# Two expert blocks at 240 columns, an earlier normalisation of 16 rows, and a conditional block laid out behind its empty side

## The chip, the cores and the metric

One core of a Trainium2 chip runs the kernel. The time is device time in microseconds of one execution; the number that counts is the median of several. The profile is of one execution. Its engines are PE (TensorE, matrix products), DVE (VectorE), ACT (ScalarE), POOL (GpSimd, here mostly indirect DMAs) and SP (SyncE, which issues the weight loads). In the profile, a "q" behind an engine's name means its instruction queue.

## The reference

A pre-norm block: linear attention with a residual, then a mixture of experts of which each token uses one, with a residual. S = 2048 tokens, D = 512, 32 heads, F = 1792, E = 8 experts, all in f32.

```python
h  = x + attention(layernorm(x), wqkv, w_phi, wo)
xf = layernorm(h)
idx = argmax(xf @ w_gate)              # one expert for each token; its gate is softmax of one value, 1
out = zeros_like(xf)
for e in range(E):
    out = out + (idx == e) * (silu(xf @ w1[e]) @ w2[e])
return h + out
```

With the inputs of this case the experts 0 to 7 get 103, 594, 80, 127, 286, 222, 239 and 397 tokens.

## The kernel before

The attention is computed first. While it ends, tables are built that say which rows belong to which expert; then the experts are worked through in **stages**, each with one expert's weights. Rows are fetched from DRAM by indirect DMAs on POOL (`rows`), normalised on DVE or ACT (`norm`, `tile_n`), transposed on PE into columns (`turn`, `tile_t`), multiplied by w1 (called g1 here), passed through Silu, multiplied by w2 (g2), added to the residual (`result`) and scattered to the output.

Every product is made of three matmuls in fp32r (`mm3`), of a high and a low part of each operand: hi x hi, lo x hi, hi x lo. High parts are rounded copies made by ACT (`hi_of`, `hi_piece`), low parts are differences made by DVE (`lo_of`, `lo_piece`). The weights of an expert come in seven chunks of 1 MB into the buffers `raw[0]` to `raw[6]`, loaded by SP's queue, and are split piece by piece into `whi` and `wlo`. A `step(c, i)` in a stage's table of hooks is such a piece i of chunk c.

The stages run in this order: unit 0 (128 rows of the most loaded expert, the "star", number 1), wide S (its other 468 rows), **pair 1** and **pair 2** (256 rows each), pairs 3 to 8 (only as many as the tables call for), a wide stage of WN = 288 rows, single(0), wide U with WU = 400 rows, single(1), and singles 2 to 7, again conditional. Here wide U holds expert 7, the 288-row stage expert 4, the pairs experts 5 and 6, and the singles experts 0, 2 and 3. Pairs 3 to 8 do not run, and one conditional single does.

A pair has 14 steps j over F (NJ) and one more. In step j, g1 makes 128 rows of the hidden layer for all 256 columns of x: four k blocks of D, three matmuls each, the weights stationary and x moving. Silu on ACT and the split on ACT and DVE follow, and two steps later g2 adds their product with w2 to two halves `pl[0][:, t, :]` in PSUM, with 128 rows of tokens stationary and 512 columns of w2 moving. `todo[j]` holds what else is put into a step: gathers of the next pair, normalisations, steps of weight splitting, and the branch hint.

`tbl` is a generator that computes the tables in wide S on DVE, one part to a hook (`behind(next, tbl)`): which expert fills the wide stages (`o1`, `o0`), how many blocks each expert needs, and where the rows lie. The functions star_a to star_d behind it write the index lists, read the expert numbers into registers and issue the loads of the next unit (`load(c, nx0)`).

Order is set in three ways. Each engine runs its instructions in order. A scheduler puts them into that order by the sequence of the code and by `after(...)`, which orders but is no wait on another engine. Waits come from the data: a semaphore for each buffer's reader and writer. For a conditional block both sides are laid out in program memory, the preferred one right behind the compare; the empty side sets the semaphores as if the block had run.

In single(0), the rows of the coming wide U are prepared between pieces of g2: `tile_n(t)` normalises tile t on DVE, `tile_t(t)` transposes it on PE and splits it into `zx`. Tile 3 has 16 rows (400 - 384), gathered into `xg[0]`.

Of the kernel before, what the change touches and what calls it, by code (L numbers as in the profile page):

```python
# [41 lines left out]
ST = ((0, P), (P, P), (2 * P, P), (3 * P, WS - 3 * P))  # L42
WC = 20
# [7 lines left out]
EV = E + 1  # L51
# [7 lines left out]
def kernel(  # L59
# [62 lines left out]
    V.tensor_scalar(first[:, 1:EV], desc8, -float(NT), float(NT * E), op0=OP.mult, op1=OP.add)  # L122
# [17 lines left out]
    est1 = consts.tile([P, 1], F32, name="est1")  # L140
# [6 lines left out]
    lemask = consts.tile([P, EV, EV], F32, name="lemask")  # L147
# [30 lines left out]

    def gather(q):
        for t in range(2):  # L180
            rows(xg[2 * (q == 1) + t], 2 * q + t)
# [14 lines left out]
    def norm(g, eng, xn=None):  # L196
        xn = xn2[0] if xn is None else xn
        if eng is A:
            return A.activation(xn[:, 0:D], g[:, 0:D], AF.Identity, bias=g[:, D:D + 1], scale=g[:, D + 1:D + 2])
        return V.tensor_scalar(xn[:, 0:D], g[:, 0:D], g[:, D + 1:D + 2], g[:, D:D + 1], op0=OP.mult, op1=OP.add)  # L200

    def turn(h, l, pool=None, xn=None):
        xn = xn2[0] if xn is None else xn
        pt = pool.tile([P, 512], F32, name="mtx", tag="s") if pool else bank("mtr")
        for k in range(KD):
            pin["mtr"] = T.transpose(pt[:, k * P:(k + 1) * P], xn[:, k * P:(k + 1) * P], ident)
        ptv = pt.rearrange("p (k t) -> p k t", k=KD)
        i = hi_of(h, ptv)
        return i, lo_of(l, ptv, h)

    def turn2(q, t, pool=None):
        v = slice(t * P, (t + 1) * P)
        return turn(xhi[1 - q % 2][:, :, v], xlo[1 - q % 2][:, :, v], pool)
# [78 lines left out]
    def tables(pool):  # L292
# [9 lines left out]
        key, m8 = v8("key"), v8("m8")  # L302
        V.tensor_copy(te, ns)
        for w, o in ((WU, o1), (WN, o0)):
            V.tensor_scalar(bs, cnt, P / 2 - 0.25 - w, FLOOR, op0=OP.add, op1=OP.add)
            V.scalar_tensor_tensor(b8, bs, FLOOR, starP, op0=OP.subtract, op1=OP.max)
            V.tensor_tensor(d8, ns, b8, op=OP.subtract)
            V.tensor_tensor(key, d8, desc8, op=OP.add)
            if o is o0:
                V.scalar_tensor_tensor(key, o1, -4.0 * S, key, op0=OP.mult, op1=OP.add)  # L310
            V.max(out=m8, in_=key)
            V.tensor_scalar(o, key, m8[:, 0:1], None, op0=OP.is_ge)
            V.tensor_tensor(d8, d8, o, op=OP.mult)
            pin["lo"] = V.tensor_tensor(te, te, d8, op=OP.subtract)
            if o is o1:
                yield
        yield
        t2, pe, pn, w8, n8 = [v8(n) for n in ("t2", "pe", "pn", "w8", "n8")]
        tp, more = one("tp"), one("more")
# [6 lines left out]
        w9 = pool.tile([P, EV], F32, name="w9")  # L326
        V.scalar_tensor_tensor(ns, n8, 1.0, star, op0=OP.mult, op1=OP.mult, accum_out=nb[:, 0:1])
        V.tensor_tensor(nb[:, 1:EV], n8, ns, op=OP.subtract)
        V.tensor_reduce(tp, pn, AX.X, OP.add)
        V.scalar_tensor_tensor(more, nS, 2.0 * PT, tp, op0=OP.mult, op1=OP.subtract)  # L330
        V.scalar_tensor_tensor(nb[:, 0:1], more, 0.0, nb[:, 0:1], op0=OP.max, op1=OP.add)
        V.scalar_tensor_tensor(bs, w8, 1.0, star, op0=OP.mult, op1=OP.mult, accum_out=w9[:, 0:1])
        pin["lo"] = V.tensor_tensor(w9[:, 1:EV], w8, bs, op=OP.subtract)
# [79 lines left out]
    def flags_of(pool):  # L413
        one = lambda name: pool.tile([P, 1], F32, name=name)
        ex, junk = tb["ex"], tb["junk"]
        end = endx[:, 1:EV + 1]
        live, ce, eend, nx, cc, md, c1, own_ = [one(n) for n in ("live", "ce", "eend", "nx", "cc", "md", "c1", "ow")]
        eI = pool.tile([P, E], F32, name="eI")
        ew = pool.tile([P, 2], F32, name="ew")
        fm = tb["sT"]  # L420
        V.tensor_scalar(eI, desc8, -1.0, float(E), op0=OP.mult, op1=OP.add)
        V.tensor_scalar(c1, ex, 0.0, est1, op0=OP.is_equal, op1=OP.mult)
        V.tensor_scalar(live, pol, end[:, EV - 1:EV], None, op0=OP.is_lt)
        for i in range(2):
            V.scalar_tensor_tensor(jk, (o0, o1)[i], 1.0, eI, op0=OP.mult, op1=OP.mult, accum_out=ew[:, i:i + 1])
        V.scalar_tensor_tensor(junk[:, 0:EV], end, po, onesE[:, 0:EV], op0=OP.is_equal, op1=OP.mult, accum_out=ce)
        V.scalar_tensor_tensor(junk[:, 0:EV], slots[:, 0:EV], ex, end, op0=OP.is_equal, op1=OP.mult, accum_out=eend)
        V.tensor_tensor(own_, c1, ex, op=OP.add)
# [3 lines left out]
        V.tensor_scalar(fm[:, 96:97], own_, 1.0, float(E - 1), op0=OP.subtract, op1=OP.min)  # L432
# [18 lines left out]
    with ExitStack() as actx:  # L451
# [608 lines left out]
        def s_star():  # L1060
# [8 lines left out]
            V.tensor_scalar(est1, m[:, 1:2], -1.0, float(E + 1), op0=OP.mult, op1=OP.add)  # L1069
            V.tensor_scalar(est16, m[:, 1:2], float(-NT), float(E * NT), op0=OP.mult, op1=OP.add)  # L1070
            V.tensor_scalar(first[:, 0:1], m[:, 1:2], float(-NT), float(E * NT + 4), op0=OP.mult, op1=OP.add)
# [274 lines left out]
    def pair_result():  # L1346
        for t in range(2):
            result(LC + 1 + t, pl[0][:, t, :], xg[2 + t])
# [9 lines left out]
    def result(col, py, g):  # L1358
        pin["y"] = V.scalar_tensor_tensor(g[:, 0:D], py, g[:, D + 2:D + 3], g[:, 0:D], op0=OP.mult, op1=OP.add)  # L1359
        scatter(g, col)  # L1360
# [66 lines left out]
    def pair(q, hooks=None):  # L1427
# [6 lines left out]
        py = []  # L1434

        def g2(i, t):
            v = slice(t * P, (t + 1) * P)
            with after(pin["g1"]):
                pin["g2"] = mm3(py[t], rh[i % 3][:, v], rl[i % 3][:, v], w2_at(whi, i), w2_at(wlo, i), i == 0, i == NJ - 1)

        def ahead(t):
            with after(pin["hi"]), after(pin["lo"]):
                pin["lo"] = norm(xg[t], V)
# [66 lines left out]
    def single(r):  # L1510
# [55 lines left out]
        if r == 0:  # L1566
# [6 lines left out]
            with after(h2), after(x2):  # L1573
# [114 lines left out]
    def star_n(t):  # L1688
        with after(pin["lo"]):
            pin["lo"] = norm(xg[2 + t], V)  # L1690

    def star_x(t):
# [5 lines left out]
        3: [behind(next, tbl), star_a], 4: [star_b, star_c], 5: [star_f, star_d] + [call(rows, xrS[t], t, ST[t][1], gidS) for t in range(3)],  # L1698
# [19 lines left out]
    with ExitStack() as ictx:  # L1718
        for q in range(3, NP + 1):
            ictx.enter_context(tc.If(np_v > 2 * (q - 1), preferred_fallthrough_block=True, label=f"p{q}"))  # L1720
# [16 lines left out]
    pair_result()  # L1737
# [77 lines left out]
```

## Time and profile before

| what | value |
|---|---|
| time, median of 3 runs | 625.16 us (624.47 to 625.37) |
| the profiled execution: its time, its span, its mean clock | 624.18 us, 622.5 us, 0.998 |
| pair 1, first matmul to the next stage's first | 353.7 to about 396.2 us |
| pair 2 | about 396.2 to 438.5 us |
| wide stage of 288 rows | 438.5 to 483.8 us |
| single(0) | 483.8 to 509.5 us |
| matmul rows of g1 in the two pairs, 128x256 | 6 groups of 56 |

A timeline row of the profile reads: start in us, duration in us, engine, line of the kernel, operation, what is written <- what is read, shapes, type and count, and in brackets how long the engine stood idle before it and what released it. Rows of one line give the duration in ns (least, median, most) and the first and last start. In a by-form row the numbers behind the bar are the busy time in us and the mean duration in ns. Durations of matmuls overlap, since the next one starts while the last drains; the distance between starts is what a matmul costs.

### The profile page before, as it was taken

The numbers are of one execution on the slowest core, as the hardware profiler recorded it, in microseconds if no ns is written. First come the engines' busy times: TensorE is split into PE (matmuls) and PEld (weight loads), VectorE is DVE, ScalarE is ACT, GpSimd is POOL, SyncE is SP. The second block draws the span as 40 slices with busy tenths as digits, with TensorE's granted clock in tenths as the row PEclk, the third lists the DMA queues.
The fourth block names the chain that finished last, engine by engine and source line by source line (L and its number), as shares of the span: only waits on it lengthen the run. The fifth ranks groups of instructions, "written<-read, shape, count | busy, mean of one in ns | idle before, by whom it ended". The sixth has DMA issues, their size and how long they took to land. (4 is left out here: it accounts for less than half of the span.)

```text
span 622.5 us, 13751 instructions
## 1 busy us (share of the span) xinstructions
PE 612.6 (98%) x5213; PEld 549.1 (88%) x5213; DVE 437.5 (70%) x902; ACT 355.5 (57%) x626; POOL 238.9 (38%) x333
## 2 busy tenths in 40 slices
PE   9999999999999999999999999999999999999996
PEld 8888888888889999888888999989999879999884
DVE  7988786878898878985434657776555784446992
ACT  6666766667534537872234546666456655645781
POOL 5587788877706645541200012230401430010420
PEclk9999999999999999999999999999999999999999
DMA  8712111210103249631294276574756584444930
GB/s 312 265 37 54 50 53 52 53 52 20 35 10 96 81 153 386 232 80 51 76 411 135 68 287 264 199 249 148 263 177 195 179 303 158 135 170 143 339 126 20
DMA packets 25118, 95.20 MB, mean 153 GB/s; under 512 B 3844, under 2 KB 3844, under 8 KB 17872
## 3 DMA queue, kind: packets, MB, share of 16 engines
q1 hardware_dynamic: 20624, 80.81, 37.1%
q0 software_dynamic: 4272, 13.38, 6.6%
q8 instruction: 44, 0.72, 0.5%
q14 instruction: 34, 0.28, 0.1%
q10 hardware_dynamic: 144, 0.02, 0.0%
HBM read 85.77 MB, written 8.68 MB: 152 GB/s over the span
## 5 line engine op out<-in xcount | busy, mean ns | idle before, releaser
L244 DVE TENSOR_TENSOR wlo<-raw,whi 128x1024 fp32r<-128x1024 f32 (+1 forms) x119 | 135.2, 1159 | 25.2 <-ACT whi L87 24.7
L87 ACT ACTIVATE whi<-raw 128x1024 fp32r<-128x1024 f32 (+1 forms) x120 | 115.0, 992 | 3.2 <-issue 1.6
L176 POOL DMA_INDIRECT xg<-hbuf,gidx x26 | 32.4, 1246 | 124.7 <-DVE xn L200 49.2
L93 PE MATMUL gw<-zx,whi 128*128 128x256 f32 (+3 forms) x212 | 69.8, 329 | 0.0
L699 POOL TENSOR_TENSOR ph<-t,sm 128x1024 f32<-128x1024 f32 x32 | 62.1, 1942 | 16.9 <-DVE sm L697 16.5
L95 PE MATMUL gw<-zx,wlo 128*128 128x256 f32 (+3 forms) x212 | 68.6, 323 | 0.0
L94 PE MATMUL gw<-zx,whi 128*128 128x256 f32 (+3 forms) x212 | 68.5, 323 | 0.0
L90 DVE TENSOR_TENSOR hA<-hs,hA 128x256 fp32r<-128x256 f32 (+3 forms) x57 | 27.2, 478 | 58.6 <-ACT hA L87 56.7
L1313 ACT ACTIVATE hs<-gw 128x468 f32<-128x468 f32 (+2 forms) x39 | 19.2, 493 | 76.2 <-PE gw L95 73.9
L93 PE MATMUL yt<-hA,whi 128*128 128x468 f32 (+2 forms) x168 | 56.7, 338 | 0.0
L95 PE MATMUL yt<-hA,wlo 128*128 128x468 f32 (+2 forms) x168 | 56.7, 338 | 0.0
L696 DVE TENSOR_REDUCE sm<-t 128x64 f32<-128x1024 f32 x32 | 38.9, 1215 | 20.0 <-ACT t L691 18.0
L691 ACT ACTIVATE t<-t,rstd 128x1024 f32<-128x1024 f32 x32 | 36.8, 1151 | 27.2 <-DVE t L690 24.7
L93 PEld LDWEIGHTS gw<-zx,whi 128*128 128x128 f32 x212 | 39.9, 188 | 2.1 <-ACT hs L1313 0.4
L94 PEld LDWEIGHTS gw<-zx,whi 128*128 128x128 f32 x212 | 40.0, 189 | 1.5
L95 PEld LDWEIGHTS gw<-zx,wlo 128*128 128x128 f32 x212 | 39.9, 188 | 1.3
L190 POOL DMA_INDIRECT out_dram<-xg,sidx x13 | 14.5, 1119 | 65.7 <-DVE xg L1359 31.4
L94 PE MATMUL yt<-hA,whi 128*128 128x288 f32 (+2 forms) x116 | 37.8, 326 | 0.0
L93 PE MATMUL po<-wohi,xh 128*128 128x260 f32 x128 | 37.5, 293 | 0.1
L95 PE MATMUL po<-wohi,xl 128*128 128x260 f32 x128 | 36.6, 286 | 0.1
L94 PE MATMUL po<-wolo,xh 128*128 128x260 f32 x128 | 36.1, 282 | 0.0
L87 ACT ACTIVATE hA<-hs 128x256 fp32r<-128x256 f32 (+3 forms) x70 | 33.8, 483 | 2.2
(466 smaller groups left out, 1785.9 us busy)
## 6 DMA issues: line engine op xcount, KB each, us to landing
raw<-in_w_dram SPq DMA_DIRECT2D x56, 1024.0 KB, 6.6
xt<-in_x_dram SPq DMA_DIRECT2D x32, 256.0 KB, 3.1
xT<-in_xTs_dram SPq DMA_DIRECT2D x16, 256.0 KB, 2.7
hbuf<-hb SPq DMA_DIRECT2D x6, 515.0 KB, 4.5
hbuf<-hb SPq DMA_DIRECT2D x2, 514.0 KB
phT<-in_wv_dram SPq DMA_DIRECT2D x4, 256.0 KB, 3.3
phT<-in_wqkT_dram SPq DMA_DIRECT2D x4, 256.0 KB, 5.5
phT<-in_wqkT_dram SPq DMA_DIRECT2D x2, 512.0 KB
```

The lines of the kernel that those rows point to most:

```text
L87: return A.activation(dst, src, AF.Copy)
L90: return V.tensor_tensor(dst, src, hi.bitcast(F32), op=OP.subtract)
L93: T.matmul(ps, ahi, bhi, start=first, stop=False)
L94: T.matmul(ps, ahi, blo, start=False, stop=False)
L95: return T.matmul(ps, alo, bhi, start=False, stop=last)
L176: G.indirect_dma_start(out=dst[0:n, :], out_offset=None, in_=hbuf if col or tab is gidS else hbuf[0:S // 2, :], in_offset=bass.IndirectOff ...
L190: m = G.indirect_dma_start(out=out, out_offset=bass.IndirectOffsetOnAxis(ap=tab[0:n, col:col + 1], axis=0), in_=src[0:n, 0:D], in_offset=N ...
L244: return eng.tensor_tensor(lo, r, h.bitcast(F32), op=OP.subtract)
L691: pin["ex"] = A.activation(t, t, AF.Exp, scale=st[c]["rstd"])
L696: V.tensor_reduce(sm, t, AX.X, OP.add)
L699: pin["f2"] = G.tensor_tensor(ph.rearrange("p (a f) -> p a f", f=DH), t, bc(sm, DH), op=OP.mult)
L1313: A.activation(h, p, AF.Silu)
```

## The change

There are four parts.

**240 columns.** A constant PN = 240 is added, and pairs 1 and 2 pass 240 columns instead of 256: 128 and 112 rows. Gathers, normalisations, transposes, g1, Silu, splits, the second half of g2 and the results shrink to that (`pair_n`). In pair 2 the last 32 rows of the second half of `pl` are set to zero at its start.

**The tables.** So that two experts fit into 240, the tables choose them as they choose those of the wide stages: two more rounds of the loop over (WU, o1), (WN, o0), now also (PN, o2), (PN, o3), with a running `used`. The lists grow by three entries (EV = E + 4), the experts are named by a table `eid`, and the tables need one hook more, so star_a to star_d each stand one step later. The mask `lemask` is no longer a constant made at the start but a scratch tile in `raw[0]`, made on POOL at the end of the attention. For the inputs here the two experts are 5 and 6, as before, and the number of blocks of every kind is unchanged.

**Late rows.** In single(0), `tile_n(3)` stands before the split of chunk 0 instead of behind tile 2.

**The conditional pair 3.** The If of pair 3 prefers the empty side behind the compare, and its hint is inverted to match.

The core of the diff:

```diff
+PN = 240
-EV = E + 1
+EV = E + 4
...
+    def pair_n(q, t):
+        return (PN if q < 3 else PT) - P if t else P
...
-        for w, o in ((WU, o1), (WN, o0)):
+        for w, o in ((WU, o1), (WN, o0), (PN, o2), (PN, o3)):
...
-            if o is o0:
-                V.scalar_tensor_tensor(key, o1, -4.0 * S, key, op0=OP.mult, op1=OP.add)
+            if o is not o1:
+                V.scalar_tensor_tensor(key, used, -4.0 * S, key, op0=OP.mult, op1=OP.add)
...
+        V.scalar_tensor_tensor(key, te, 1.0 / P, first[:, 4:EV], op0=OP.mult, op1=OP.add)
+        for i, o in enumerate((o2, o3)):
+            V.scalar_tensor_tensor(bs, o, 1.0, key, op0=OP.mult, op1=OP.mult, accum_out=w9[:, 1 + i:2 + i])
+            pin["lo"] = V.scalar_tensor_tensor(b8, o, 1.0, eid[:, 4:EV], op0=OP.mult, op1=OP.mult,
+                                               accum_out=eid[:, 1 + i:2 + i])
...
-                f"p{q + 1}", hint=smin(smax(vals["p"] - 2 * q, 0), 1),
+                f"p{q + 1}", hint=smin(smax(2 * q + 1 - vals["p"] if q == 2 else vals["p"] - 2 * q, 0), 1),
...
+        if q == 2:
+            V.memset(pl[0][P - 32:P, 1, :], 0.0)
...
-                        pin["g1"] = mm3(p, w1_at(whi, c, k)[:, o:o + P], w1_at(wlo, c, k)[:, o:o + P], own_x[0][:, k, :],
-                            own_x[1][:, k, :], k == 0, k == KD - 1)
+                        pin["g1"] = mm3(p, w1_at(whi, c, k)[:, o:o + P], w1_at(wlo, c, k)[:, o:o + P], own_x[0][:, k, 0:nc_],
+                            own_x[1][:, k, 0:nc_], k == 0, k == KD - 1)
...
                 h2, x2 = tile_t(0, ws[0], xU, UT)
-            with after(h2), after(x2):
+            with after(x2):
+                n = tile_n(3, ws[3], UT)
+            with after(h2), after(n):
                 split_chunk(0)
...
                 h2, x2 = tile_t(2, ws[2], xU, UT)
-                with after(pin["lo"]):
-                    tile_n(3, ws[3], UT)
...
-        3: [behind(next, tbl), star_a], 4: [star_b, star_c], 5: [star_f, star_d] + [call(rows, xrS[t], t, ST[t][1], gidS) for t in range(3)],
+        3: [behind(next, tbl)], 4: [behind(next, tbl), star_a], 5: [star_b, star_c], 6: [star_f, star_d] + [call(rows, xrS[t], t, ST[t][1], gidS) for t in range(3)],
...
-            ictx.enter_context(tc.If(np_v > 2 * (q - 1), preferred_fallthrough_block=True, label=f"p{q}"))
+            ictx.enter_context(tc.If(np_v > 2 * (q - 1), preferred_fallthrough_block=q > 3, label=f"p{q}"))
```

How it moves instructions is seen in the order of the program, where a row is a line, an operation, what it writes <- what it reads, and a shape. On PE, at the end of pair 2, before: the last g2, the compare for pair 3, and then the body of pair 3.

```order
L93 MATMUL pl<-whi_4553,hA 128x512
L94 MATMUL pl<-wlo_4554,hA 128x512
L95 MATMUL pl<-whi_4553,hA 128x512
L1718 COMPARE_AND_BRANCH
L1254 UNCONDITIONAL_BRANCH
L1256 UNCONDITIONAL_BRANCH
```

Now the compare is followed by the empty side, which ends with a branch, and the body of pair 3 comes behind it:

```order
L94 MATMUL pl<-whi_4554,hA 112x512
L95 MATMUL pl<-wlo_4555,hA 112x512
L96 MATMUL pl<-whi_4554,hA 112x512
L1735 COMPARE_AND_BRANCH
L1735 UNCONDITIONAL_BRANCH
L1268 UNCONDITIONAL_BRANCH
L1270 UNCONDITIONAL_BRANCH
```

The other end of both jumps lies some 1,780 such rows further on PE, behind the bodies of pairs 3 to 8, at the first matmul of the 288-row stage. Before, the seven branches that end the innermost body and the six empty sides stood there, pair 3's the last of them:

```order
L93 MATMUL pl<-whi_4553,hA 128x512
L94 MATMUL pl<-wlo_4554,hA 128x512
L95 MATMUL pl<-whi_4553,hA 128x512
L1718 UNCONDITIONAL_BRANCH x7
L93 MATMUL mh<-zx,whi_3702 128x288
```

Now six branches are left at that place; the empty side of pair 3, whose branch goes to the same matmul, is the one that was shown behind the compare. The other engines have the same layout.

On DVE, in single(0), before: `zx` 128x4x128 are the low parts of tiles 0 to 2, the row 16x512 is `tile_n(3)`, `wlo` are weight pieces, and `zx` 128x4x16 is tile 3.

```order
L90 TENSOR_TENSOR zx<-mtr,zx 128x4x128
L244 TENSOR_TENSOR wlo_3703<-raw_3524,whi_3702 128x1024 x2
L90 TENSOR_TENSOR zx<-mtr,zx 128x4x128
L244 TENSOR_TENSOR wlo_3709<-raw_3527,whi_3708 128x1024
L90 TENSOR_TENSOR zx<-mtr,zx 128x4x128
L1279 TENSOR_SCALAR xg_3710<-xg_3710 16x512
L90 TENSOR_TENSOR zx<-mtr,zx 128x4x16
```

Now:

```order
L91 TENSOR_TENSOR zx<-mtr,zx 128x4x128
L1293 TENSOR_SCALAR xg_3711<-xg_3711 16x512
L251 TENSOR_TENSOR wlo_3704<-raw_3524,whi_3703 128x1024 x2
L91 TENSOR_TENSOR zx<-mtr,zx 128x4x128
L251 TENSOR_TENSOR wlo_3710<-raw_3527,whi_3709 128x1024
L91 TENSOR_TENSOR zx<-mtr,zx 128x4x128
L91 TENSOR_TENSOR zx<-mtr,zx 128x4x16
```

The 16x512 row has moved ahead of three weight pieces and of tiles 1 and 2; nothing else changed its place there.

More of the change, by code (lines that the diff above doesn't have):

```diff
@@ L121 @@
     first = consts.tile([P, EV], F32, name="first")
-    V.tensor_scalar(first[:, 1:EV], desc8, -float(NT), float(NT * E), op0=OP.mult, op1=OP.add)
+    V.memset(first[:, 0:3], 0.0)
+    V.tensor_scalar(first[:, 4:EV], desc8, -float(NT), float(NT * E), op0=OP.mult, op1=OP.add)
+    eid = consts.tile([P, EV + 1], F32, name="eid")
+    V.tensor_scalar(eid[:, 4:EV], desc8, -1.0, float(E), op0=OP.mult, op1=OP.add)
+    V.memset(eid[:, EV:EV + 1], 0.0)
     blk0 = consts.tile([P, EV + 1], F32, name="blk0")
@@ L177, in rows @@
                              in_offset=bass.IndirectOffsetOnAxis(ap=tab[0:n, col:col + 1], axis=0))
+    def pair_n(q, t):
+        return (PN if q < 3 else PT) - P if t else P
     def gather(q):
         for t in range(2):
-            rows(xg[2 * (q == 1) + t], 2 * q + t)
+            rows(xg[2 * (q == 1) + t], 2 * q + t, pair_n(q, t))
     def own(r):
@@ L204, in turn @@
         pt = pool.tile([P, 512], F32, name="mtx", tag="s") if pool else bank("mtr")
+        n = h.shape[2]
         for k in range(KD):
-            pin["mtr"] = T.transpose(pt[:, k * P:(k + 1) * P], xn[:, k * P:(k + 1) * P], ident)
-        ptv = pt.rearrange("p (k t) -> p k t", k=KD)
+            pin["mtr"] = T.transpose(pt[:, k * n:(k + 1) * n], xn[0:n, k * P:(k + 1) * P], ident[0:n, 0:n])
+        ptv = pt[:, 0:KD * n].rearrange("p (k t) -> p k t", k=KD)
         i = hi_of(h, ptv)
@@ L211, in turn2 @@
     def turn2(q, t, pool=None):
-        v = slice(t * P, (t + 1) * P)
+        v = slice(t * P, t * P + pair_n(q, t))
         return turn(xhi[1 - q % 2][:, :, v], xlo[1 - q % 2][:, :, v], pool)
@@ L301, in tables @@
         V.scalar_tensor_tensor(ns, ns, FLOOR, starP, op0=OP.subtract, op1=OP.max)
-        key, m8 = v8("key"), v8("m8")
+        key, m8, used, o2, o3 = [v8(n) for n in ("key", "m8", "used", "o2", "o3")]
+        w9 = pool.tile([P, EV], F32, name="w9")
+        V.memset(w9[:, 0:1], 0.0)
+        lemask = pool.tile([P, EV, EV], F32, name="lemask")
+        G.memset(lemask, 1.0 / P)
+        G.affine_select(out=lemask, in_=lemask, compare_op=OP.is_ge, fill=0.0, base=0,
+                        pattern=[[1, EV], [-1, EV]], channel_multiplier=0)
         V.tensor_copy(te, ns)
-        for w, o in ((WU, o1), (WN, o0)):
+        for w, o in ((WU, o1), (WN, o0), (PN, o2), (PN, o3)):
             V.tensor_scalar(bs, cnt, P / 2 - 0.25 - w, FLOOR, op0=OP.add, op1=OP.add)
@@ L308, in tables @@
             V.tensor_tensor(key, d8, desc8, op=OP.add)
-            if o is o0:
-                V.scalar_tensor_tensor(key, o1, -4.0 * S, key, op0=OP.mult, op1=OP.add)
+            if o is not o1:
+                V.scalar_tensor_tensor(key, used, -4.0 * S, key, op0=OP.mult, op1=OP.add)
             V.max(out=m8, in_=key)
             V.tensor_scalar(o, key, m8[:, 0:1], None, op0=OP.is_ge)
+            if o is o1:
+                V.tensor_copy(used, o)
+            elif o is not o3:
+                V.tensor_tensor(used, used, o, op=OP.add)
             V.tensor_tensor(d8, d8, o, op=OP.mult)
             pin["lo"] = V.tensor_tensor(te, te, d8, op=OP.subtract)
-            if o is o1:
+            if o is o1 or o is o0:
                 yield
+        V.scalar_tensor_tensor(key, te, 1.0 / P, first[:, 4:EV], op0=OP.mult, op1=OP.add)
[3 more added lines that the diff above has]
+                                               accum_out=eid[:, 1 + i:2 + i])
         yield
         t2, pe, pn, w8, n8 = [v8(n) for n in ("t2", "pe", "pn", "w8", "n8")]
-        tp, more = one("tp"), one("more")
         V.tensor_tensor(t2, te, starP, op=OP.subtract)
@@ L325, in tables @@
         V.tensor_scalar(w8, pe, 2 * FLOOR, isP, op0=OP.subtract, op1=OP.mult)
[L326 to L333, printed above, removed]
+        V.tensor_scalar(nb[:, 0:3], nS.to_broadcast([P, 3]), float(PT), None, op0=OP.mult)
+        V.memset(nb[:, 0:1], 0.0)
+        V.scalar_tensor_tensor(ns, n8, 1.0, star, op0=OP.mult, op1=OP.mult, accum_out=nb[:, 3:4])
+        V.tensor_tensor(nb[:, 4:EV], n8, ns, op=OP.subtract)
+        V.scalar_tensor_tensor(bs, w8, 1.0, star, op0=OP.mult, op1=OP.mult, accum_out=w9[:, 3:4])
+        pin["lo"] = V.tensor_tensor(w9[:, 4:EV], w8, bs, op=OP.subtract)
         yield
@@ L416, in flags_of @@
         end = endx[:, 1:EV + 1]
-        live, ce, eend, nx, cc, md, c1, own_ = [one(n) for n in ("live", "ce", "eend", "nx", "cc", "md", "c1", "ow")]
-        eI = pool.tile([P, E], F32, name="eI")
+        live, ce, eend, nx, cc, md, own_, nid = [one(n) for n in ("live", "ce", "eend", "nx", "cc", "md", "ow", "nid")]
         ew = pool.tile([P, 2], F32, name="ew")
         fm = tb["sT"]
-        V.tensor_scalar(eI, desc8, -1.0, float(E), op0=OP.mult, op1=OP.add)
-        V.tensor_scalar(c1, ex, 0.0, est1, op0=OP.is_equal, op1=OP.mult)
         V.tensor_scalar(live, pol, end[:, EV - 1:EV], None, op0=OP.is_lt)
         for i in range(2):
-            V.scalar_tensor_tensor(jk, (o0, o1)[i], 1.0, eI, op0=OP.mult, op1=OP.mult, accum_out=ew[:, i:i + 1])
+            V.scalar_tensor_tensor(jk, (o0, o1)[i], 1.0, eid[:, 4:EV], op0=OP.mult, op1=OP.mult, accum_out=ew[:, i:i + 1])
         V.scalar_tensor_tensor(junk[:, 0:EV], end, po, onesE[:, 0:EV], op0=OP.is_equal, op1=OP.mult, accum_out=ce)
         V.scalar_tensor_tensor(junk[:, 0:EV], slots[:, 0:EV], ex, end, op0=OP.is_equal, op1=OP.mult, accum_out=eend)
-        V.tensor_tensor(own_, c1, ex, op=OP.add)
+        V.scalar_tensor_tensor(junk, slots, ex, eid, op0=OP.is_equal, op1=OP.mult, accum_out=own_)
         V.tensor_copy(ewi, ew)
@@ L1068, in s_star @@
             V.tensor_scalar(esti, m[:, 1:2], -1.0, float(E), op0=OP.mult, op1=OP.add)
-            V.tensor_scalar(est1, m[:, 1:2], -1.0, float(E + 1), op0=OP.mult, op1=OP.add)
+            for i in (0, 3):
+                V.tensor_scalar(eid[:, i:i + 1], m[:, 1:2], -1.0, float(E), op0=OP.mult, op1=OP.add)
             V.tensor_scalar(est16, m[:, 1:2], float(-NT), float(E * NT), op0=OP.mult, op1=OP.add)
-            V.tensor_scalar(first[:, 0:1], m[:, 1:2], float(-NT), float(E * NT + 4), op0=OP.mult, op1=OP.add)
+            V.tensor_scalar(first[:, 3:4], m[:, 1:2], float(-NT), float(E * NT + 4), op0=OP.mult, op1=OP.add)
             V.tensor_scalar(star, sc, m[:, 1:2], None, op0=OP.is_equal)
@@ L1344, with pair_result @@
     we, yl, pl, vals = [], [], [], {}
-    def pair_result():
+    def pair_result(q):
         for t in range(2):
-            result(LC + 1 + t, pl[0][:, t, :], xg[2 + t])
+            result(LC + 1 + t, pl[0][:, t, :], xg[2 + t], pair_n(q, t))
     def last_result(r=None):
@@ L1356, in last_result, with result @@
                 rows(xg[0], SB + r)
-    def result(col, py, g):
-        pin["y"] = V.scalar_tensor_tensor(g[:, 0:D], py, g[:, D + 2:D + 3], g[:, 0:D], op0=OP.mult, op1=OP.add)
-        scatter(g, col)
+    def result(col, py, g, n=P):
+        pin["y"] = V.scalar_tensor_tensor(g[0:n, 0:D], py[0:n], g[0:n, D + 2:D + 3], g[0:n, 0:D], op0=OP.mult, op1=OP.add)
+        scatter(g, col, n)
     def half(c, i):
@@ L1434, in pair @@
         py = []
+        nc_ = P + pair_n(q, 1)
         def g2(i, t):
-            v = slice(t * P, (t + 1) * P)
+            v = slice(t * P, t * P + pair_n(q, t))
             with after(pin["g1"]):
-                pin["g2"] = mm3(py[t], rh[i % 3][:, v], rl[i % 3][:, v], w2_at(whi, i), w2_at(wlo, i), i == 0, i == NJ - 1)
+                pin["g2"] = mm3(py[t][0:pair_n(q, t)], rh[i % 3][:, v], rl[i % 3][:, v], w2_at(whi, i), w2_at(wlo, i), i == 0, i == NJ - 1)
         def ahead(t):
             with after(pin["hi"]), after(pin["lo"]):
-                pin["lo"] = norm(xg[t], V)
+                pin["lo"] = norm(xg[t][0:pair_n(q + 1, t)], V)
         def turned(t):
@@ L1458, in keep @@
                 for t in range(2):
-                    rows(xg[2 + t], 2 * q + t)
+                    rows(xg[2 + t], 2 * q + t, pair_n(q, t))
         if q == 1:
@@ L1736 @@
         load(c, es0)
-    pair_result()
+    pair_result(NP)
     wide({
```

27 lines of the change are left out of this document (11 added, 16 removed).

## The prediction

> **What bounds the kernel now.** I read the page first: its head, the busy shares and the row of the granted clock; then the timeline of PE in the stages that the change touches.
>
> ```profile
> span 622.5 us, 13751 instructions
> PE 612.6 (98%) x5213; PEld 549.1 (88%) x5213; DVE 437.5 (70%) x902; ACT 355.5 (57%) x626; POOL 238.9 (38%) x333
> PEclk9999999999999999999999999999999999999999
> ```
>
> PE has work in 98% of the span, at the full clock in every slice, and no other engine is above 70%. So a microsecond taken off PE's stream in the mixture-of-experts part comes off the time, one added to it is added, and what another engine does counts only where PE waits for it. The change touches three places of that stream: the matmuls of pairs 1 and 2, the branch behind pair 2, and the transposes in single(0). The profiled execution took 624.18 us, 1.7 more than its span; the median of the runs is 625.16, 0.98 higher. I work out changes to 624.18 and add 0.98 at the end.
>
> **Part 1: 240 columns.** The first matmul of each pair (g1) streams 256 columns of x; now 240. In each pair that is 14 steps of 4 x 3 matmuls, 168, so 336 in all; the three lines carry 56 each.
>
> ```profile
> L93 PE MATMUL gw<-xhi,whi 128*128 128x256 f32 x56 | 16.3, 291 | 0.0
> ...
> 398.73 0.28 PE L93 MATMUL gw<-zx,whi 128*128 128x256 f32 x1
> ...
> 400.41 0.28 PE L95 MATMUL gw<-zx,wlo 128*128 128x256 f32 x1
> ...
> 436.69 0.40 PE L93 MATMUL pl<-whi,hA 128*128 128x512 f32 x1
> ...
> 437.85 0.40 PE L95 MATMUL pl<-whi,hA 128*128 128x512 f32 x1
> ...
> 439.82 0.30 PE L93 MATMUL mh<-zx,whi 128*128 128x288 f32 x1
> ...
> 441.00 0.30 PE L93 MATMUL gw<-zx,whi 128*128 128x288 f32 x1
> ```
>
> The durations overlap; what counts is the distance of starts. From 398.73 to 400.41 there are 14 steps: 0.120 us for 256 columns. From 439.82 to 441.00 there are 9: 0.131 for 288. From 436.69 to 437.85 there are 5: 0.232 for 512. So a column costs 0.35 ns between 256 and 288 and 0.45 between 288 and 512. Sixteen columns at these slopes are 5.6 to 7.2 ns. But no matmul of this type with fewer than 256 columns is in the trace, and each one also loads 128 columns of weights. Does that load allow less than 0.12? The nearest rows:
>
> ```profile
> 6.93 0.28 PE L93 MATMUL pv<-wvhi,xh 128*128 128x260 f32 x1
> ...
> 9.34 0.28 PE L95 MATMUL pv<-wvhi,xl 128*128 128x260 f32 x1
> ...
> 13.19 3.06 PE L611 MATMUL pf<-wphi_s,phT 128*128 128x128 f32 x26
> ...
> L611 PE MATMUL pf<-wphi_s,phT 128*128 128x128 f32 x64 | 7.5, 275 | 0.0
> ```
>
> 260 columns came every 0.1205 (20 steps), hardly more than 256: the curve is flattening. Against that, 26 records of the plain-f32 type, each with its own load of 128 columns, came within 3.06 us, the last lasting 0.275: 25 steps of 0.111. A load per 0.111 is possible, then. I take 0.113 to 0.114, 6.5 ns less than now: 336 x 6.5 = **-2.2 us**. Ends: 0 (a floor at 0.12) and 336 x 9 = -3.0 (the 0.111 of the f32 rows). The second matmul (g2) still streams 512 columns, so its 112 stationary columns take nothing off. Silu, splits and gathers get shorter beside a saturated PE: nothing.
>
> [...]
>
> **Part 2: the branch behind pair 2.** With four blocks p3 is not run. Before, the compare jumps far, to the empty side, which lies right ahead of the next stage, and a hint placed in pair 2 names that side. Now the empty side follows the compare, but it ends with an unconditional jump over six pair bodies, and the hint concerns the compare only. The rows of the branch line (queue rows, "q"), then PE's matmuls around it:
>
> ```profile
> L1718 ACTq COMPARE_BRANCH  x1: 74/74/74, 435.0 to 435.0; - x1
> L1718 PEldq COMPARE_BRANCH  x1: 396/396/396, 435.8 to 435.8; - x1
> L1718 ACTq EVENT_SEMAPHORE  x1: 17/17/17, 435.9 to 435.9; - x1
> ...
> L1718 PEldq EVENT_SEMAPHORE  x1: 51/51/51, 438.3 to 438.3; - x1
> ...
> 438.54 0.37 PE L93 MATMUL mh<-zx,whi 128*128 128x288 f32 x1 [0.30 <-PEq L1718]
> ```
>
> PE's compare ran at 435.8, 2.4 us ahead of the array; what stops PE is the semaphore instruction on the empty side, which stands at 438.3, just as the last matmul of pair 2 (the row at 437.85 above, 0.40 long) ends. The gap of starts is 0.69 where 512 columns need 0.23: 0.46 lost, and all of it is this drain. The new layout has the same semaphore instruction, so the 0.46 stays, and behind it, with the array empty, comes the new jump. Its price if the target is at hand: the last single has such a short jump.
>
> ```profile
> L1765 PEldq COMPARE_BRANCH  x3: 73/195/355, 590.7 to 616.7; - x3
> ...
> L1765 PEldq EVENT_SEMAPHORE  x1: 51/51/51, 616.5 to 616.5; - x1
> ...
> L1811 PEldq DRAIN  x2: 8/8/8, 616.9 to 622.0; - x2
> ```
>
> Semaphore 616.5, jump 616.7, next instruction 616.9: about 0.25 us more than without a jump. Its price if the instructions must first be fetched is shown by ACT after the branch:
>
> ```profile
> L1313 ACTq EVENT_SEMAPHORE  x1: 3183/3183/3183, 437.2 to 437.2; - x1
> ...
> q14 instruction: 1, 0.01, 4.7%
> ...
> q8 instruction: 1, 0.02, 4.2%
> ```
>
> ACT left the empty side at 435.9 and did nothing until 437.2; in between one instruction packet moved (the stretch 436.0 to 436.7: 4.7% of 16 engines x 0.7 us = 0.53 us). From its jump at 435.0 to the first instruction from the new page: 2.2 us. PE's packet is larger (stretch 437.3 to 438.6: 4.2% x 16 x 1.3 = 0.87 us), so on PE 2.2 + 0.35, about 2.5. I take **+2.5 us**; ends +0.25 and +3.0 (half a microsecond above, as the jump can start only after the drain). The other engines jump too, but ACT then waited 3.2 us for PE anyway, so 2.2 fits there. A chance that the fetch is started earlier remains, as no row shows an unhinted far jump: rival B.
>
> [...]
>
> **Part 3: late rows sooner.** tile_n(3) normalises 16 rows on DVE; it moves from behind zx tile 2 to right behind zx tile 0.
>
> ```profile
> 498.82 0.88 POOL L176 DMA_INDIRECT xg<-hbuf,gidx  x1 [4.08 <-DMA out_dram<-xg,sidx]
> ...
> q0 software_dynamic: 16, 0.03, 2.2%
> ...
> q0 software_dynamic: 16, 0.00, 1.6%
> ...
> 501.47 0.69 DVE L90 TENSOR_TENSOR zx<-mtr,zx 128x512 fp32r<-128x512 f32 x1 [0.49 <-ACT zx L87]
> 502.42 2.36 DVE L244 TENSOR_TENSOR wlo<-raw,whi 128x1024 fp32r<-128x1024 f32 x2 [0.26 <-ACT whi L87]
> ...
> 507.03 0.56 DVE L1279 TENSOR_SCALAR xg<-xg 16x512 f32<-16x512 f32 x1
> 508.38 0.23 DVE L90 TENSOR_TENSOR zx<-mtr,zx 128x64 fp32r<-128x64 f32 x1 [0.79 <-ACT zx L87]
> ...
> 506.16 0.40 PE L95 MATMUL my<-whi,zx 128*128 128x512 f32 x1
> 507.69 0.39 PE L1286 MATMUL mtr<-ident,xg 16*128 16x16 f32 x4 [1.13 <-issue]
> ...
> 509.51 0.34 PE L93 MATMUL mh<-zx,whi 128*128 128x400 f32 x1
> ```
>
> PE stood from 506.16 + 0.23 to 507.69 for the normalised rows: 1.3 us. But their gather was issued at 498.82; its 16 data packets (0.03 MB) moved between 499.7 and 503.2, and its 16 closing packets between 503.2 and 504.4. A DVE that comes to tile_n(3) at 502.1 waits until about 504.2, with both wlo pieces (2.36) and three zx rows queued behind it. From 504.2: 0.45 + 2.36 + 0.6 (zx 1) + 1.15 (wlo) + 0.6 (zx 2) + 0.25 (zx 3) gives 509.6. Wide U's first matmul, at 509.51 now, needs all of zx. So PE's wait moves and does not go: **+0.1**, between -1.3 (the rows land early) and +0.5.
>
> **Part 4: the rest.** About 25 small table operations on DVE lengthen the choice of experts by one step of wide S, so the loads of the next unit are issued a step later.
>
> ```profile
> 314.56 0.56 ACT L1313 ACTIVATE hs<-gw 128x468 f32<-128x468 f32 x1 [3.88 <-PE gw L95]
> 315.15 0.60 ACT L87 ACTIVATE hA<-hs 128x468 fp32r<-128x468 f32 x1
> 315.65 1.04 ACT L87 ACTIVATE whi<-raw 128x1024 fp32r<-128x1024 f32 x1
> 319.68 0.56 ACT L1313 ACTIVATE hs<-gw 128x468 f32<-128x468 f32 x1 [2.98 <-PE gw L95]
> ```
>
> A step is 319.68 - 314.56 = 5.1 us. The first piece on ACT (315.65) then has its chunk up to 5.1 later, about 320, and holds the activation of 319.68 back by up to 1.4 us. ACT has 3 to 4 us of waiting for PE in each step, and PE has the next step's first matmuls (12 of 468 columns, by the slope above 0.21 each, 2.5 us) before it needs that result: 0, at worst +1. The mask built later on POOL and the clearing of 32 rows of pl on DVE (0.56 at most, as the 16-row operation above) lie on engines with 62% and 30% free: 0, at worst +0.5.
>
> Sum: -2.2 + 2.5 + 0.1 = **+0.4**; 624.6, and beside the median 625.5. I say 625.4.
>
> **Rivals.** A is this forecast.
>
> B, the jump is cheap: the fetch of its target has begun by the time the array drains, and the step costs 0.25. For it: no row shows an unhinted far jump, so the fetch of 2.2 us is carried over from another case. Against it: nothing in the program names the target ahead of the jump, and ACT's row shows no fetch before the need. -2.2 + 0.25 + 0.1 = -1.85, **623.3**.
>
> C, slower: the weight load is the bound of g1, so its spacing stays near 0.12 (place: the 336 matmuls of both pairs; price: the 2.2 us do not come, while the jump is paid; it decides from a spacing above 0.117). For it: 256 and 260 columns stand at the same 0.120. Against it: the f32 rows at 0.111. 0 to -0.8, + 2.5 + 0.1: **627 to 627.8**.
>
> D, below 256 columns this type falls to the rate of plain f32. By the rows above, two records of 0.111 per 128 columns make 0.42 for 240, 0.3 more, x 336 = +100: **725**. For it only that the trace has no narrower one; against it the smooth fall of the spacing from 512 to 256.
>
> E, the late rows do land in time and PE's 1.3 us goes: **624.1** with A's other terms. Against it: the closing packets after 503.2. That the edit of part 3 changes nothing is A itself.
>
> **Numbers.** A 0.47, B 0.28, C 0.14, D 0.04, E 0.07. From 622.6 to 627.0 lie nearly all of A (624.5 to 626.4) and E, most of B and the near edge of C: a little over 0.8. A measurement here tells 0.2%, 1.25 us, from no change: faster means under 623.9, slower over 626.4. Faster: most of B, slivers of A and E, 0.27. Slower: D, most of C, a tail of A, 0.20. Same: 0.53.
>
> **What would show it.** In the changed profile: g1 starts 0.113 to 0.114 apart in both pairs (0.12 is C, 0.4 is D); behind pair 2 a gap of some 3 us on PE with an instruction packet in it (0.9 is B); in single(0) DVE idle before the 16x512 row, and PE waiting at wide U's first matmul instead of at the transposes; the first whi piece of wide S near 320 with no gap on PE. I am wrong if the gap behind pair 2 is under 1 us, or if PE waits in wide S.

## The result, and the profile after

| | before | after | ratio (95% interval) |
|---|---|---|---|
| median of the runs | 624.92 us | 631.45 us | 1.0105 (1.0088 to 1.0123) |
| the profiled execution: span, mean clock | 622.5 us, 0.998 | 629.5 us, 0.991 | |

The kernel became 6.5 us slower; 625.4 had been forecast, with 627.0 as the upper end. Ratios leave out one execution of a later run (the row behind tile 1), which took 1233.14 us at a granted clock of 0.49. The page of the changed kernel, its head, the busy shares and the granted clock:

```profile
span 629.5 us, 13796 instructions
PE 613.6 (97%) x5213; PEld 548.0 (87%) x5213; DVE 440.7 (70%) x937; ACT 354.6 (56%) x626; POOL 239.7 (38%) x333
...
PEclk9999999999999999999999999999799999999998
```

PE's busy time is as before, but in one slice of forty, 441 to 456 us, the clock is at 0.7 (the 8 of the last slice lies behind PE's last matmul, which ends at 623.5: over 626.3 to 627.3 the clock is 0.50). The timeline of PE shows that place: the last matmuls of pair 2, and the first of the 288-row stage.

```profile
435.85 0.40 PE L96 MATMUL pl<-whi,hA 128*112 128x512 f32 x1
442.63 0.58 PE L94 MATMUL mh<-zx,whi 128*128 128x288 f32 x1 [6.38 <-issue]
443.00 0.44 PE L95 MATMUL mh<-zx,whi 128*128 128x288 f32 x1
443.24 0.44 PE L96 MATMUL mh<-zx,wlo 128*128 128x288 f32 x1
```

The distance of starts is 6.78 us; before it was 0.69. Behind the gap the same matmuls come every 0.24 us instead of 0.13. The rows of the branch line say what filled the gap:

```profile
L1735 ACTq COMPARE_BRANCH  x2: 34/36/38, 432.9 to 434.0; - x2
L1735 PEldq COMPARE_BRANCH  x2: 103/3065/6027, 433.9 to 436.4; - x2
...
L1735 PEldq EVENT_SEMAPHORE  x1: 51/51/51, 436.3 to 436.3; - x1
```

The compare at 433.9 took 0.1 us. The empty side's semaphore instruction ran at 436.3, as the array drained; then the unconditional jump, which the profile also calls a compare, took 6.03 us. The busy time of the engines by stretch, with the granted clock in the third column from the end, then the DMA share and GB/s:

```profile
436.10:442.60 6.50, 0.14 (x1) 0.00 (x1) 1.41 (x2) 0.00 (x0) 3.10 (x4) 0.89 0.95 349
442.60:447.80 5.20, 5.17 (x21) 5.20 (x22) 0.46 (x1) 0.86 (x2) 1.44 (x3) 0.50 0.45 173
447.80:455.00 7.20, 7.20 (x53) 7.00 (x53) 3.82 (x5) 5.08 (x9) 0.68 (x1) 0.99 0.32 81
```

After 6.4 us without a matmul PE ran at half clock (0.50) for 5.2 us. From the first matmul of each stage to that of the next, the two profiles compare like this:

| stretch of PE | before | after | difference |
|---|---|---|---|
| start to wide S | 280.43 | 281.08 | +0.65 |
| wide S | 73.28 | 72.86 | -0.42 |
| pair 1 | 42.50 | 41.56 | -0.94 |
| pair 2, first to last matmul | 41.64 | 40.35 | -1.29 |
| last matmul of pair 2 to the next stage | 0.69 | 6.78 | **+6.09** |
| stage of 288 rows | 45.29 | 47.84 | **+2.55** |
| single(0) | 25.68 | 24.55 | -1.13 |
| wide U | 61.70 | 63.02 | +1.32 |
| singles 1 and 2, to the last matmul | 44.89 | 45.06 | +0.17 |

The sum is +7.0, the difference of the spans. The two bold rows are 8.6 us. Of the stage of 288 rows, 0.2 us is there in the later runs without the half clock too (45.47). Why wide S became 0.42 us shorter was not followed up.

### The profile page after: what moved, and what is told of

It is laid out like the page before. It is cut to its first block, busy times and chain, and to the rows that moved or that the text cites. A ratio compares the mean times of both kernels' runs of the same rounds, so it can differ in the third digit from the quotient of the medians.

```text
span 629.5 us, 13796 instructions
## 1 busy us (share of the span) xinstructions
PE 613.6 (97%) x5213; PEld 548.0 (87%) x5213; DVE 440.7 (70%) x937; ACT 354.6 (56%) x626; POOL 239.7 (38%) x333
## 5 line engine op out<-in xcount | busy, mean ns | idle before, releaser
L94 PE MATMUL gw<-zx,whi 128*128 128x240 f32 (+3 forms) x212 | 69.9, 329 | 0.0
L95 PE MATMUL gw<-zx,whi 128*128 128x240 f32 (+3 forms) x212 | 68.6, 324 | 0.0
L96 PE MATMUL gw<-zx,wlo 128*128 128x240 f32 (+3 forms) x212 | 68.5, 323 | 0.0
L91 DVE TENSOR_TENSOR hA<-hs,hA 128x240 fp32r<-128x240 f32 (+3 forms) x57 | 26.7, 469 | 56.5 <-ACT hA L88 55.2
L88 ACT ACTIVATE hA<-hs 128x240 fp32r<-128x240 f32 (+3 forms) x70 | 33.4, 478 | 2.2
```

The costliest lines, as they stand in the source:

```text
L88: return A.activation(dst, src, AF.Copy)
L91: return V.tensor_tensor(dst, src, hi.bitcast(F32), op=OP.subtract)
L94: T.matmul(ps, ahi, bhi, start=first, stop=False)
L95: T.matmul(ps, ahi, blo, start=False, stop=False)
L96: return T.matmul(ps, alo, bhi, start=False, stop=last)
```

## The experiments

**The layout undone.** Pair 3 laid out and hinted as before, all else of the change kept:

```diff
-hint=smin(smax(2 * q + 1 - vals["p"] if q == 2 else vals["p"] - 2 * q, 0), 1)
+hint=smin(smax(vals["p"] - 2 * q, 0), 1)
-preferred_fallthrough_block=q > 3, label=f"p{q}"
+preferred_fallthrough_block=True, label=f"p{q}"
```

> The changed kernel with the If of pair 3 laid out and hinted as before; all else of the change stays. Theory (the far jump is the whole loss): the gap behind pair 2 falls from 6.8 us to 0.7, the half clock behind it goes, so 631.5 - 6.1 - 2.5 = 622.8 us, 2 us under the kernel before, with g1 0.113 to 0.116 apart. Rival (the tables' extra step or the columns cost as well): 624 to 627 us, with a gap of PE in wide S or g1 at 0.12.

It took 623.48 us; ratio to the kernel before 0.9972 (0.9961 to 0.9983). PE at the end of pair 2:

```profile
436.51 0.40 PE L96 MATMUL pl<-whi,hA 128*112 128x512 f32 x1
437.21 0.37 PE L94 MATMUL mh<-zx,whi 128*128 128x288 f32 x1 [0.30 <-PEq L1735]
```

The gap behind pair 2 is 0.70 us again and the 288-row stage takes 45.47. So the layout alone accounts for the loss, and the rest of the change is a gain of 0.3%. The second try:

> The first run's kernel (pair 3 laid out as before, all else of the change) once more. Theory: 622.5 to 623.9, 0.2 to 0.4% under the kernel before, single(0) and wide U together within 0.5 us of the kernel before. Rival (the first result was its chip's): no difference from the kernel before.

623.48 again, 0.9978 (0.9968 to 0.9988), with single(0) and wide U 88.13 us together against 87.38 before: 0.75 over, more than the 0.5 expected.

**The layout alone**, in the kernel before (the same lines, the other way round).

> The kernel before with nothing but the new layout and hint of pair 3's If. Theory (the jump alone does it): a gap of 6 to 7 us behind pair 2 and about 5 us of half clock after it, 625 + 8.6 = 633.5 us. Rival (it takes the other parts too, since they move what SP loads at that time): a gap under 4 us, under 630 us.

632.89 us in one run, and the jump on PE took 6.10 us; the 288-row stage behind it took 47.35 against 45.29. The jump needs none of the other parts.

**Two weight loads left out.** In the changed kernel, the two loads that SP issues just behind the branch:

```diff
     load_flags(NQ)
-    for c in (2, 3):
-        load(c, es0)
     pair_result(NP)
```

> The changed kernel without the two 1 MB weight loads that SP issues just behind the branch (chunks 2 and 3 of the single's expert are left out, so single(0) multiplies with stale weights there). Theory Q (PE's instruction page waits in the DMA queues behind these loads): the jump falls from 6.0 us to 2.5 to 3.3, and the time to 626 to 628. Theory F (an unfetched jump costs PE 6 us whatever else moves): the jump stays between 5.5 and 6.5 us, the time near 631.5.

629.78 us in one run; the jump took 4.53 us. Neither theory was right: the loads make up 1.5 of the 6.0 us, and 4.5 are left without them.

**The same jump where DMA is quiet.** Pair 3 as before, and single 3, which does not run either, laid out behind its empty side:

```diff
-hint=smin(smax(vals["s"] - (r + 1), 0), 1)
+hint=smin(smax(r + 2 - vals["s"] if r == 2 else vals["s"] - (r + 1), 0), 1)
-preferred_fallthrough_block=True, label=f"s{r}"
+preferred_fallthrough_block=r != 3, label=f"s{r}"
```

> The kernel of the first run (pair 3 as before), with the If of single 3, which does not run either, laid out and hinted the way the change did it for pair 3: the same kind of jump at the end of the program, where no weight loads are under way. Theory (PE's unhinted jump costs about 4.5 us by itself, and loads add the rest): PE's jump takes 4.2 to 4.8 us there. Rivals: 6 us again (loads have nothing to do with it), or 2.5 us as on ACT (all above that is traffic). PE has no work behind it; the end moves only as far as DVE's own jump (3 us, from about 613.4) passes PE's last matmul: 0.5 to 1.5 us over the first run.

624.07 us in one run, 0.6 over the first run; behind PE's last matmul the profile is only 0.3 us longer, less than expected. The jump on PE took 3.29 us, between the 2.5 of one rival and the 4.2 to 4.8 of the theory.

**The old layout with the wrong hint.** The changed kernel with only the layout undone, so that the hint of pair 3 now names the side that is not taken.

> The changed kernel with pair 3 laid out as before, but with the changed hint, which now names the wrong side: a far jump by the compare, unhinted. Theory (what costs is the page that nothing asked for ahead): PE's compare, which runs 2 us ahead of the array, takes 4.5 to 6 us, and the gap behind pair 2 is 2.5 to 4.5 us. Rival (it is the unconditional jump, or its place behind the drained semaphore, that is slow): the gap is 0.7 us as in the first run, 623.5 us.

The timeline of PE in this kernel, and its rows of the branch line:

```profile
436.05 0.40 PE L96 MATMUL pl<-whi,hA 128*112 128x512 f32 x1
437.92 0.37 PE L94 MATMUL mh<-zx,whi 128*128 128x288 f32 x1 [1.47 <-PEq L1735]
```

```profile
L1735 ACTq COMPARE_BRANCH  x1: 50/50/50, 433.1 to 433.1; - x1
L1735 PEldq COMPARE_BRANCH  x1: 3509/3509/3509, 434.1 to 434.1; - x1
...
L1735 ACTq EVENT_SEMAPHORE  x1: 17/17/17, 435.5 to 435.5; - x1
```

PE's compare took 3.51 us; it had taken 0.40 with the right hint. Most of it lies ahead of the drain, so the gap is 1.87 us and not 6.8, and the one run took 624.85. The rival is out: a jump by the compare was slow too, 3.51 us, when nothing had asked for its target. The size expected for it was too large.

The five jumps stand together in the next views. For the changed kernel, the layout alone, the two loads left out, the wrong hint and the last jump, each row is the stretch from PE's jump to the start of the packet that brings its instructions (that start is read from the trace's list of DMA packets; for the last jump it is 617.07); the last two columns are the DMA share and GB/s.

```profile
436.50:440.10 3.60, 0.00 (x0) 0.00 (x0) 1.27 (x2) 0.00 (x0) 0.94 (x1) 1.00 0.88 345
```

```profile
439.00:442.70 3.70, 0.00 (x0) 0.00 (x0) 1.41 (x2) 0.00 (x0) 0.95 (x1) 1.00 0.93 352
```

```profile
436.40:438.50 2.10, 0.00 (x0) 0.00 (x0) 0.06 (x1) 0.00 (x0) 0.95 (x1) 1.00 0.60 151
```

```profile
434.10:435.10 1.00, 1.00 (x6) 0.76 (x5) 1.00 (x1) 0.00 (x0) 0.00 (x0) 1.00 0.06 16
```

```profile
616.10:617.20 1.10, 0.00 (x0) 0.00 (x0) 0.75 (x1) 0.00 (x0) 0.00 (x0) 1.00 0.08 22
```

And the jumps themselves: with the layout alone, without the two loads, and at the end of the program.

```profile
L1718 PEldq COMPARE_BRANCH  x2: 103/3102/6102, 436.3 to 438.9; - x2
```

```profile
L1735 PEldq COMPARE_BRANCH  x2: 103/2318/4532, 433.8 to 436.4; - x2
```

```profile
L1782 PEldq COMPARE_BRANCH  x3: 71/73/3285, 590.0 to 616.1; - x3
```

With the DMA engines 6 to 8% busy the packet starts 1.0 us after the jump and the jump takes 3.3 to 3.5; at 60% 2.1 and 4.5; at 88% 3.6 and 6.0; at 93% 3.7 and 6.1. What follows the packet's start is much the same each time, 2.3 to 2.5 us. So the bare price on PE is about 3.4 us here, and the rest goes with the later start of the packet. That the two loads take 1.5 us of it is shown by leaving them out; that the gathers and scatters of the same moment make the other 1.1 is an argument from the shares, and was not tried.

**Columns.** Only 128 of the 240 columns in g1, Silu and splits of both pairs; the other 112 rows of each get stale values.

```diff
-        nc_ = P + pair_n(q, 1)
+        nc_ = 128 if q < 3 else PT
```

> The kernel of the first run with the changed layout of pair 3 and only 128 of the 240 columns in the first matmul, Silu and splits of pairs 1 and 2 (the other 112 rows of each are left out and get stale values). It measures how far the distance of matmuls falls below 256 columns. If the columns alone set it: 0.45 ns a column, 0.062 to 0.066 us. If the load of 128 weight columns sets a floor: 0.10 to 0.112, which for 240 columns would leave nothing more to gain by narrower blocks.

Pair 3 is laid out as in the first run here, not in the changed layout that the expectation names. 622.46 us in one run. First and last of 16 steps in the changed kernel at 240 columns, then of 19 steps here at 128:

```profile
397.62 0.27 PE L95 MATMUL gw<-zx,whi 128*128 128x240 f32 x1
...
399.40 0.27 PE L96 MATMUL gw<-zx,wlo 128*128 128x240 f32 x1
```

```profile
397.15 0.27 PE L95 MATMUL gw<-zx,whi 128*128 128x128 f32 x1
...
399.26 0.28 PE L96 MATMUL gw<-zx,wlo 128*128 128x128 f32 x1
```

Both are 0.111 us. These are stretches of g1 alone; where g1 comes in groups of twelve between g2, the third to the last start lie 0.1125 us apart at 240 columns and 0.112 at 128 (0.1196 at 256, in the kernel before). So 240 columns stand on the floor already. At 128 columns some matmuls at the start of a group follow after 0.05 to 0.06 us, but then the first g2 starts later, and pair 2 takes 41.06 us in place of 41.04. Pair 1 takes 41.12 in place of 41.62; that half microsecond was not followed up. The other way, 256 columns again (16 with stale values that nothing reads), with all else of the first run:

```diff
-        nc_ = P + pair_n(q, 1)
+        nc_ = PT
```

> The kernel of the first run, but g1, Silu and splits of pairs 1 and 2 run over 256 columns again (16 columns with stale values are added, nothing reads them). Tables, gathers, transposes and the moved row stay. Theory (the saving is the 336 matmuls): g1 back at 0.1195, 2.2 to 2.4 us over the first run, 625 to 626. Rival (the saving came from the shorter rows around them): within 0.8 us of the first run.

626.55 us, ratio 1.0020 (1.0007 to 1.0033). Pair 1 takes 42.52 and pair 2 42.10 (41.62 and 41.04 in the first run): the columns are worth 2.0 us. The medians lie another 1.1 us apart. That goes with two waits that this profile has and the first run's has not: 0.35 us in wide S, where the first weight piece on ACT is late and holds an activation back, and 1.2 us in the 288-row stage.

**The late rows.** tile_n(3) at its old place, with the layout of the first run:

```diff
-            with after(x2):
-                n = tile_n(3, ws[3], UT)
-            with after(h2), after(n):
+            with after(h2), after(x2):
                 split_chunk(0)
...
                 h2, x2 = tile_t(2, ws[2], xU, UT)
+                with after(pin["lo"]):
+                    tile_n(3, ws[3], UT)
```

> The kernel of the first run with tile_n(3) at its old place, behind the zx row of tile 2: the 240 columns and the tables alone. Theory (the move of the change only shifts PE's wait into wide U): within 0.5 us of the first run, 623 to 624, with 1.3 us of wait at the 16-row transposes and none at wide U's first matmul. Rival (the move gained): 0.8 us or more above the first run.

623.04 us, 0.9971 (0.9960 to 0.9982); PE waits 1.3 us at the 16-row transposes, and wide U's first matmuls run on. The move of the change gains nothing. Then the row between the two places, behind tile 1:

```diff
                 h2, x2 = tile_t(1, ws[1], xU, UT)
+            with after(x2):
+                n = tile_n(3, ws[3], UT)
-            with after(h2), after(x2):
+            with after(h2), after(n):
                 half(3, 1)
```

> As the first of these runs, with tile_n(3) behind the zx row of tile 1 on DVE, where its rows have landed (504.2 in the trace of before, that place 505.3). Theory (the wait was the landing, and PE's stall the row's place): PE waits neither at the 16-row transposes nor at wide U's first matmul, 1.1 to 1.3 us under the first of these runs, about 621.6. Rival (DVE's own chain is late, the wait moves again): within 0.4 us of the first of these runs.

622.22 us, 0.9958 (0.9941 to 0.9976), and in its profile PE waits at neither place. The same kernel a second time:

> The version with tile_n(3) behind the zx row of tile 1 and pair 3 laid out as before, once more, since one of its runs was far out. Theory (PE's wait for the late rows is gone): 621.6 to 622.4 us, 0.35 to 0.5% under the kernel before. Rival (the first result was its chip's): 623 or more.

623.53 us, 0.9977 (0.9968 to 0.9987). The row of DVE in this second profile:

```profile
507.05 0.53 DVE L1293 TENSOR_SCALAR xg<-xg 16x512 f32<-16x512 f32 x1 [1.71 <-DMA xg<-hbuf,gidx]
```

Here the gather landed at 507.0; in the first profile the row's operation stands at 504.13 and waits for nothing. PE's 1.3 us are back. The profiled execution, 624.62 us, is the slowest of its ten, so the profile does not say how often the rows land late. The place behind tile 1 gains about 1.1 us in an execution in which the rows land in time. The three places of the row, without the far jump and at 240 columns, were measured five times in all: 0.9958 to 0.9978, with overlapping intervals. Which place is best is not settled. All five are faster than the kernel before and than the changed kernel.

A second profile of the kernel before, for the two waits seen with 256 columns, which the second profile of the row behind tile 1 has as well:

> The kernel before, unchanged, for a second profile. It tells what two waits belong to that two other profiles showed and the first ones did not: 0.36 us of PE in wide S and 1.2 us in the 288-row stage. If they come from the table change: neither is here. If they come and go with the execution: the one in the 288-row stage can be here too, and wide S takes 73.3 us as in the first profile.

Neither wait is in it: wide S 73.29 and the 288-row stage 45.27, as in the first. The wait in wide S is understood (below); that in the 288-row stage, seen in two profiles taken on one chip one after the other and in none of the rest, stays open.

## Why the prediction was wrong

**What bounds the kernel** was right: the stretches of PE's stream in the table above add up to the whole difference of the spans.

**Part 1** was right in size. Forecast -2.2 us; measured -0.94 and -1.29 in the two pairs, 2.0 us by the run with 256 columns. The distance at 240 is 0.1125 in the groups of twelve, close to the forecast 0.113 to 0.114, and 0.111 in the longest stretch, the value of the plain-f32 rows that stood as the lower end. It is a floor here: at 128 columns the same two distances are 0.112 and 0.111.

**Part 2** is the step that failed, by its size. The mechanism of the gap held in each link: the drain stays (the semaphore at 436.3), the jump comes behind it (436.4), nothing asked for its target, and PE stands still for its 6.03 us, in which the instruction packet moves (from 440.1). The term was "2.2 + 0.35, about 2.5", with 3.0 as the end; it measured 6.09. Another 2.55 us came in the stage behind it, for which the sum had no term. The signs named for being wrong looked for a gap under 1 us and not for a long one. Three things were missing:

- The bare price on PE is 3.3 to 3.5 us, not 2.5. It was carried over from ACT, where I counted from the compare. But that compare was hinted, and ACT's semaphore on the empty side ran at 435.9, before the stretch in which the packet moved, so the 2.2 us were not the price of an unhinted jump. That they come close to ACT's own price, 2.4 (433.1 to 435.5 in the run with the wrong hint), is luck, and even this is not PE's price.
- The fetch goes through the DMA engines, and SP issues two loads of 1 MB just then, at 435.4 and 436.1: they waited 3.7 us for DVE's side of the same branch. With the DMA engines 88% busy the jump took 2.6 us more than the bare 3.4; these loads are 1.5 of it. The prediction read the packet's size from two quiet stretches and did not ask what else moves at 436.
- After the 6.4 us without a matmul PE came back at half clock (0.50). Before, no gap was longer than 1.6 us in this part, and the sum had no term for the clock. About 21 matmuls at 0.24 in place of 0.13 are 2.3 of the 2.55 us.

Rival B, the cheap jump, is out. So is the half of C that would have cost most: the floor exists, but at 0.111 to 0.1125 and not at 0.12, and the saving was 2.0 to 2.2 us and not 0 to 0.8. No run shows the 0.8 us in C's sum; the runs show these 2.0 to 2.2 in its place. D is out, and so is E: the rows landed late.

**Part 3** was right. In the changed kernel, DVE and PE in single(0) and wide U:

```profile
508.11 0.69 DVE L91 TENSOR_TENSOR zx<-mtr,zx 128x512 fp32r<-128x512 f32 x1 [0.49 <-ACT zx L88]
510.94 0.53 DVE L1293 TENSOR_SCALAR xg<-xg 16x512 f32<-16x512 f32 x1 [2.15 <-DMA xg<-hbuf,gidx]
...
512.84 0.40 PE L96 MATMUL my<-whi,zx 128*128 128x512 f32 x1
513.17 0.42 PE L1300 MATMUL mtr<-ident,xg 16*128 16x16 f32 x4
...
515.02 0.34 PE L94 MATMUL mh<-zx,whi 128*128 128x400 f32 x1
516.27 0.45 PE L95 MATMUL mh<-zx,whi 128*128 128x400 f32 x1 [0.91 <-DVE zx L91]
```

DVE waits 2.15 us for the rows, the transposes follow at once, and PE's wait comes back at wide U: -1.13 and +1.32.

**Part 4** held with less room than it gave. The first piece of wide S on ACT now waits for its chunk:

```profile
315.11 0.56 ACT L1327 ACTIVATE hs<-gw 128x468 f32<-128x468 f32 x1 [4.01 <-PE gw L96]
315.70 0.59 ACT L88 ACTIVATE hA<-hs 128x468 fp32r<-128x468 f32 x1
320.33 1.06 ACT L88 ACTIVATE whi<-raw 128x1024 fp32r<-128x1024 f32 x1 [4.04 <-DMA raw<-in_w_dram]
321.30 0.54 ACT L1327 ACTIVATE hs<-gw 128x468 f32<-128x468 f32 x1
```

The piece starts at 320.3, and the activation at 321.3, ready about 1 us earlier by its step of 5.1. PE ran on. In the second profile of the row behind tile 1 the chunk came 1.1 us later (321.43); the activation was then about 2.1 us late, and PE waited 0.36 us. So about 1.7 us of delay are covered, and 1 us of them is used up. The first stretch, up to wide S, was 0.3 to 1.3 us longer in the profiles of kernels with the new tables than in the two of the kernel before (280.4 and 280.7), but the layout alone, without new tables, has 280.9. Most of it is there by 54 us, in the attention, long before a table is built. Its cause is open.

## What to carry to other kernels

A jump over code that does not run cost the fetch of its target here, 3.3 to 6.1 us on PE, unless something had asked for the target ahead (0.4 us); on the engine that bounds the kernel, let a hinted compare make that jump, and let it run while the array still has work. Price such a stall where it stands: what loads start at that moment (1.5 us here), and what the clock does after it (2.3 us here). PE's wait for the late rows was gone in one profile, where their instruction stood earlier and found them landed; where it stood ahead of the landing, the wait only moved (-1.13 and +1.32 us).

## What the runs showed of the hardware

- A jump to instructions that nobody asked for took PE 3.3 and 3.5 us with the DMA engines 6 to 8% busy, 4.5 at 60%, and 6.0 to 6.1 us with them about 90% busy. Where a hint had named the target, PE's far compare took 0.4 and no such wait is seen.
- PE came back at a clock of 0.50 after 6.4 us without a matmul, and at 0.57 over as long a stretch after 4.9 us without one (the two loads left out); after 1.5 us (the wrong hint) it stayed at 1.00. With the two loads left out, the gap and the stretch behind it read:

```profile
436.00:441.00 5.00, 0.17 (x1) 0.00 (x0) 1.41 (x2) 0.00 (x0) 2.27 (x3) 0.77 0.42 114
441.00:446.20 5.20, 5.14 (x24) 5.17 (x25) 0.46 (x1) 0.86 (x2) 2.02 (x3) 0.57 0.27 97
```

  If the clock was either full or half, a mean of 0.77 over the first 5.0 us means half clock for 2.3 of them, so from about 438.7, some 2.5 us after the last matmul ended (436.2). By the same reckoning the 0.89 over the 6.5 us of the changed kernel puts its fall at 441.2, 4.9 us after the last matmul (436.25). Behind the last matmul of the whole program (it ends at 616.5 in the kernel before, at 623.5 in the changed one) the clock was 0.74 over 618.9 to 619.9 in the kernel before and 0.57 over 625.3 to 626.3 in the changed one: a fall after 2.9 and 1.9 us. So a gap of 3 us, as it was forecast, could have met it too; this is an estimate from these four falls, and no run has such a gap between two matmuls.
- Matmuls of the fp32r type with 128 stationary columns came every 0.111 us at 240 and at 128 columns, 0.120 at 256 and at 260. At these two widths below 256 there is no fall to a slower rate, and from 240 to 128 hardly any gain (0.1125 to 0.112 in the groups of twelve).
